# Fixed engine queues, a later load of the weights, and unread matrix products in a fused Fourier-filter and gated-causal-convolution kernel

## The chip, the core and the metric

The kernel runs on one core of a Trainium2 chip. The metric is device time in microseconds (us) from the start to the end of the program, the median of the runs that were made. Five engines work side by side, each on its own instruction queue in the order written there: TensorE (PE, matrix products), VectorE (DVE), ScalarE (ACT), GpSimd (POOL, here mostly an issuer of loads) and SyncE (SP, here an issuer of stores and of transfers through a scratch in DRAM). An engine waits for another only where an instruction has to.

## The reference

`x` is 8 batches of 3200 rows by 256 channels in float32. First each channel is filtered along the rows in the frequency domain; then a causal convolution of five taps gives a gate that multiplies a projection.

```
X = rfft(x, axis=1);  y = irfft(X * (filt_r + 1j*filt_i), n=3200, axis=1)
gate = sigmoid(sum_k conv_w[k] * y[s-4+k])        # per channel, rows before 0 are zero
out  = (gate * (y @ w_val)) @ w_out               # 256 x 256 each
```

## The kernel before

The rows are split as 3200 = 100 x 32, and the transform is done by products with tables of sines that the kernel makes itself. The program is a list of small tasks, named here as in the code with batch `b` and part:

- `lx` (POOL, line 286) loads an eighth of a batch of x into one of ten buffers `xt`. `s1` (PE, line 548) is the first transform step, 8 per batch; `so` copies its result out of PSUM. `t` (DVE, line 567) transposes, 4 per batch.
- `s2` (PE, line 577) is the second step, 7 per batch; `xs` copies it out; `z` (DVE, line 593) multiplies by the filter tile `f_t`; `ia` (PE, line 608) goes back; `ue` copies it out to the tile `u`.
- Batch 0 (`TURN`) is then transposed on DVE, `k` (line 649, 4 parts, output `vt`); the other batches go through a scratch in DRAM (`wr`, `lv` on SP, `escr`).
- `ib` (PE, line 659, 8 per batch) ends the inverse transform; `ye` (ACT, line 668) copies it to `yt`. Then for 7 blocks of rows: `cv` (convolution, PE, line 698 or 712), `ga` (sigmoid, ACT, line 722), `vl` (PE, line 732, with `wv_t`), `gv` (DVE, line 747), `op` (PE, line 755, with `wo_t`), `oe` (copy), `st` (store, SP, line 770).
- Once, at the start: `wd`, `wa` make the table `w_t`; `tp` (PE, line 455) and `te` make `a_t` and `b_t` from it, 4 and 8 tasks; `cid`, `cia`, `cim` make `ci_t`; `dg` makes the convolution's diagonals on ACT. The 24 transfers of the filter (`f_t`, lines 346 to 352) are followed by eight copies `fd`, which double it across partitions, four for its first part and four for its second.

The copies `so`, `xs`, `ue`, `oe`, `te` and `fd` can run on ACT (line 539, or 469) or on DVE (line 541). PSUM is one tile of four slots of two banks; a product into a slot waits until the slot's last content has been copied out.

What comes after what on an engine is decided while the program is built. `Plan` (line 126) holds for each task its engines with estimated costs, what it depends on, which buffers it takes and gives, and a rank from the list `TIMES`. `run` steps through an imagined time: whenever an engine is free it takes, among the tasks that are ready by the estimates, the one of the lowest rank (with an addition `STAY` where PE changes its kind of product, and `LEAN` where DVE takes a copy). The tasks are then emitted in that order under a manual schedule, so each engine's queue is fixed, and on the chip each instruction waits for its true inputs.

In that order POOL issues the loads of x for batch 0, those of the filter, the first load of batch 1 (`lx1,0`), then all eleven transfers of `wv_t` and `wo_t` (one task, `load_w`, line 356), and then the other loads of batch 1. PE has `s1` of batch 1's second eighth (`s11,1`) ahead of five of batch 0's seven `ia`.

Of the kernel before, what the change touches and what calls it, by code (L numbers as in the profile page):

```python
# [24 lines left out]
STAY, LEAN = 2.6, 5.1  # L25

TIMES = [6045, -2430, 3242, -301, 64, -3062, 3825, -4640, -1646, -3299, -5370, 2181, -2530, 351,
# [90 lines left out]
NCH = R // RC  # L118
# [7 lines left out]
class Plan:  # L126
# [17 lines left out]
    def run(self):  # L144
        left = dict(self.tasks)
        users, need = {}, {}
        for n, t in left.items():
            need[n] = len(t["deps"])
            for d in t["deps"]:
                users.setdefault(d, []).append(n)  # L150
# [75 lines left out]
def kernel(  # L226
# [51 lines left out]
    st = {}  # L278
# [668 lines left out]
```

## Time and profile before

| | us |
|---|---|
| median of 3 runs | 304.4 |
| lowest, highest of the 3 | 303.82, 306.0 |
| the profiled execution | 303.57 |
| its span, first to last instruction | 301.8 |
| PE, DVE, ACT, POOL busy in it | 258.3, 263.6, 256.2, 63.0 |

The profiled execution's time is 1.8 us longer than the span between its first and last instruction. The page gives busy time by engine for the whole span and in 40 slices of 7.5 us; other views give the instructions in order of time, the busy time in chosen stretches, and the chain of waits that ended last. Tiles are called by the program's names, so `xs<-ps` is the copy of a PSUM slot to `xs`. A timeline row is start, duration, engine, line, operation, output<-input, sizes and count, and in brackets the idle time before it with what ended it. In a timeline, merged rows of a count above one run from the first start to the last end.

### The profile page before, as it was taken

Reading aid. Unit: us, or ns where it says so; the run is one execution under the profiler, and the core shown is the slowest. Engines: PE = TensorE matmul, PEld = TensorE weight load, DVE = VectorE, ACT = ScalarE, POOL = GpSimd, SP = SyncE. Lnnn points to the kernel's source line nnn. Section 1 sums busy time; section 2 is a strip of 40 time slices with the busy share of each in tenths; the row PEclk is TensorE's granted clock in tenths of the full one; section 3 lists DMA queues with packets and bytes.
Section 4 is the critical chain, followed back from the end, with each engine's and each line's share of the span. In section 5 each row is a group of like instructions: output and inputs, shape, how many; then the busy total and the mean of one; then the engine's idle time right before and its main releaser. Section 6 shows DMA issues by size and latency. Waiting matters only on the chain.

```text
span 301.8 us, 9355 instructions
## 1 busy us (share of the span) xinstructions
PE 258.3 (86%) x3924; PEld 156.8 (52%) x3924; DVE 263.6 (87%) x294; ACT 256.2 (85%) x299; POOL 63.0 (21%) x122
## 2 busy tenths in 40 slices
PE   2822492778999899989999999999999999999991
PEld 0111340634555654666466465747666677766661
DVE  7979959898999999999999999999999984766761
ACT  3997775699789997999999999999999889787652
POOL 8699953022023002300320300000000000000000
PEclk9999998799999999999999999999999999999998
DMA  6998699469689997999999997998563799875375
GB/s 91 190 112 103 79 166 186 79 94 182 173 244 269 252 305 179 222 282 359 198 237 316 289 212 205 331 311 288 174 231 121 233 292 341 280 292 208 125 292 204
DMA packets 52874, 66.00 MB, mean 219 GB/s; under 512 B 7712, under 2 KB 34208, under 8 KB 52832
## 3 DMA queue, kind: packets, MB, share of 16 engines
q1 hardware_dynamic: 40624, 50.09, 49.2%
q0 software_dynamic: 12208, 15.31, 32.7%
q8 instruction: 31, 0.51, 0.7%
q14 instruction: 11, 0.09, 0.1%
HBM read 42.54 MB, written 38.14 MB: 267 GB/s over the span
## 4 chain that ended last, share of the span: by engine, by line
PE 48%; DMA 14%; DVE 14%; POOL 9%; ACT 8%; issue 6%; SPq 0%; DVEq 0%; POOLq 0%; ACTq 0%
PE ps L755 11%; PE ps L698 11%; PE ps L732 11%; DMA vt<-escr 8%; PE ps L659 5%; PE ps L608 4%; DVE gv L747 3%; DVE so L541 3%; PE ps L712 3%; DMA out_dram<-o 3%; DMA f_t<-in_filt_r_dram 2%; PE ps L548 2%; POOL xt L286 2%; ACT so L539 2%; DVE vt L649 2%
## 5 line engine op out<-in xcount | busy, mean ns | idle before, releaser
L747 DVE TENSOR_TENSOR gv<-ps,gt 128x1024 bf16<-128x1024 f32 (+1 forms) x56 | 60.8, 1103 | 13.5 <-PE ps L732 10.1
L593 DVE TENSOR_TENSOR z<-xs,f_t 128x2048 bf16<-128x2048 bf16 (+1 forms) x56 | 62.7, 1138 | 4.3 <-ACT xs L539 4.1
L722 ACT ACTIVATE gt<-ps 128x1024 bf16<-128x1024 f32 (+1 forms) x56 | 52.1, 945 | 10.4 <-PE ps L712 5.8
L286 POOL DMA_DIRECT2D xt<-in_x_dram x64 | 36.4, 570 | 108.6 <-PE ps L548 89.3
L668 ACT ACTIVATE yt<-ps 128x800 bf16<-128x800 f32 x64 | 52.1, 846 | 7.0 <-PE ps L659 6.5
L548 PE MATMUL ps<-xt,cf_t 100*128 100x512 bf16 x128 | 43.5, 424 | 11.6 <-DMA xt<-in_x_dram 9.3
L755 PE MATMUL ps<-wo_t,gv 128*128 128x256 bf16 x400 | 51.8, 273 | 0.8 <-DVE gv L747 0.4
L732 PE MATMUL ps<-yt,wv_t 128*128 128x512 bf16 (+1 forms) x224 | 51.9, 356 | 0.0
L698 PE MATMUL ps<-yt,dg_t 64*64 64x512 bf16 (+1 forms) x880 | 48.7, 348 | 0.4
L539 ACT ACTIVATE so<-ps 128x1024 bf16<-128x1024 f32 x42 | 42.2, 1042 | 6.6 <-PE ps L548 4.2
L539 ACT ACTIVATE u<-ps 128x1024 bf16<-128x1024 f32 (+1 forms) x41 | 40.0, 982 | 4.7 <-PE ps L608 4.3
L755 PEld LDWEIGHTS <-gv 128*128 128x128 bf16 x400 | 36.8, 97 | 12.2 <-issue 3.0
L539 ACT ACTIVATE o<-ps 128x1024 f32<-128x1024 f32 (+1 forms) x37 | 36.8, 999 | 6.2 <-PE ps L755 5.3
L659 PE MATMUL ps<-ci_t,vt 104*128 104x100 f16 (+1 forms) x512 | 33.7, 213 | 8.8 <-DVE vt L649 6.5
L567 DVE STREAM_TRANSPOSE tt<-so 128x1024 f32<-128x1024 f32 x32 | 38.7, 1227 | 0.6 <-ACT so L539 0.6
L539 ACT ACTIVATE xs<-ps 128x1024 bf16<-128x1024 f32 (+1 forms) x36 | 35.3, 998 | 3.6 <-PE ps L577 3.3
L659 PEld LDWEIGHTS <-vt 104*128 104x128 bf16 (+1 forms) x512 | 28.4, 101 | 19.0 <-DVE vt L649 7.1
L698 PEld LDWEIGHTS <-dg_t 64*64 64x64 bf16 x880 | 24.3, 106 | 15.4 <-issue 4.3
L608 PE MATMUL ps<-z,a_t 64*64 64x256 bf16 x416 | 28.4, 289 | 4.5 <-ACT gt L722 1.9
L577 PE MATMUL ps<-tt,w_t 64*64 64x256 bf16 x416 | 23.5, 293 | 9.4 <-DVE tt L567 8.5
L608 PE MATMUL ps<-z,b_t 64*64 64x256 bf16 x416 | 28.1, 283 | 0.0
L732 PEld LDWEIGHTS <-wv_t 128*128 128x128 bf16 x224 | 19.0, 97 | 17.3 <-issue 3.2
(98 smaller groups left out, 225.1 us busy)
## 6 DMA issues: line engine op xcount, KB each, us to landing
out_dram<-o SPq DMA_DIRECT2D x48, 512.0 KB
xt<-in_x_dram POOLq DMA_DIRECT2D x64, 200.0 KB, 7.3
escr<-u SPq DMA_DIRECT2D x42, 256.0 KB
vt<-escr SPq DMA_DIRECT2D x56, 192.0 KB
out_dram<-o SPq DMA_DIRECT2D x8, 128.0 KB
escr<-u SPq DMA_DIRECT2D x7, 128.0 KB
vt<-escr SPq DMA_DIRECT2D x56, 16.0 KB
f_t<-in_filt_r_dram POOLq DMA_DIRECT2D x2, 112.0 KB, 3.6
```

Source lines behind the costliest of these rows:

```text
L286: nc.gpsimd.dma_start(out=xt[0:L], in_=src)
L539: nc.scalar.activation(dst, src, AF.Copy, **kw)
L548: nc.tensor.matmul(ps[:, 512 * h:512 * h + 512], lhsT=cf_t[0:L].rearrange("p h c i -> p (h c i)"), rhs=xv[:, DQ // 2 * h:DQ // 2 * h + DQ ...
L593: nc.vector.tensor_tensor(z[:, :, :, 0:nm * D], st.pop(("XS", b, u))[:, :, 0:nm * D].unsqueeze(1) .to_broadcast((128, 2, 2, nm * D)), f_t[ ...
L608: nc.tensor.matmul(ps[64 * h:64 * h + 64, 512 * t + D * a:512 * t + D * a + D], lhsT=tab[rows, h, m0 + a, :], rhs=z[rows, w, h, D * a:D * ...
L659: nc.tensor.matmul(ps[:, o:o + L], lhsT=v[rows, RC * j + a, 128 * dh:128 * dh + 128], rhs=ci_t[rows, way, :], start=True, stop=True)
L668: nc.scalar.activation(y[:, :, H:H + N].rearrange("p h (a r) -> p h a r", r=R)[:, :, :, RC * j:RC * j + RC], ps[:, :].rearrange("p (h n) - ...
L698: nc.tensor.matmul(ps[o:o + 64, 512 * dh:512 * dh + w], lhsT=dg_t[rows, dh, k, :], rhs=y[rows, dh, BLK * c + k:BLK * c + k + w], start=(k ...
L722: nc.scalar.activation(g[:, :, 0:w], two_banks(ps, w), AF.Sigmoid)
L732: nc.tensor.matmul(ps[:, 512 * eh:512 * eh + w], lhsT=wv_t[:, dh, eh, o:o + 128], rhs=y[:, dh, H + BLK * c:H + BLK * c + w], start=(dh == ...
L747: nc.vector.tensor_tensor(o, i0, i1, op=ALU.mult)
L755: nc.tensor.matmul(ps[:, D * a:D * a + D], lhsT=gv_[:, eh, 128 * a:128 * a + 128], rhs=wo_t[:, c % 2 * pair(b, c), eh, :], start=(eh == 0) ...
```

## The change

The rank list goes. `QUEUES` now lists, for each of the five engines, the numbers of its tasks in order, so that both the order and the choice between ACT and DVE are written down. `run` only works out imagined times for that order, needed for the PSUM slots, and gives start and end of each task back. The core of it:

```diff
-TIMES = [6045, -2430, 3242, ...
+QUEUES = dict(
+    PE=[0, 2, 4, 6, 8, 10, 12, 1557, 14, 1554, 1563, 21, 1560, 26, 24, 31, 36, 29, 142, ...],
+    DVE=[1549, 1551, 1553, 1566, 16, 17, 18, 19, 1543, 1540, 1542, 23, ...],
...
+WARM, COLD = 0.25, (14.0, 45.0)
...
+            for e, line in lines.items():
+                if line and free.get(e, 0.0) <= now + 1e-9 and can(line[0]):
+                    begin(line.pop(0), e)
...
+            order.append((t["emit"], e, t["slots"], now, end))
...
-    def load_w():
+    def load_wv():
         for dh in range(2):
...
+
+    def load_wo():
         for s in range(2):
...
+    def warm(us):
+        flat = w_t[...].rearrange("p s k -> p (s k)")
+        ps = psum()
+        for h in range(int(us / WARM)):
+            o = 512 * (h % 2)
+            nc.tensor.matmul(ps[:, o:o + 512], lhsT=flat[:, 0:128],
+                             rhs=flat[:, o + 128:o + 640], start=True, stop=True)
...
-            dep = dep + ([f"s1{b},{j - 1}"] if j else [])
+            dep = dep + ([f"s1{b},{j - 1}"] if j else [f"s1{b - 1},{NCH - 1}"] if b else [])
...
-    add("wts", {"POOL": 5.0}, ["pool"], lambda e: load_w())
+    add("wv", {"POOL": 4.2}, ["pool"], lambda e: load_wv())
+    dma("wvq", 2.4, ["wv"], land=2.0, mode=1)
+    add("wo", {"POOL": 3.4}, ["wv"], lambda e: load_wo())
+    dma("woq", 2.6, ["wo"], land=2.0, mode=1)
...
-        for emit, e, slots in order:
+        idle = 0.0
+        for emit, e, slots, at, end in order:
+            st["slots"] = list(slots)
+            if e == "PE":
+                if slots and COLD[0] < idle and at < COLD[1] and at - idle > WARM:
+                    warm(at - idle)
+                idle = end
```

The estimates of when x, the filter and the loads arrive are changed too; they only enter the imagined times. The first `vl` and the first `op` now depend on the loads of `wv_t` and `wo_t` in the plan. No task is added or dropped; the only new instructions are the unread products.

**The unread products.** Where the plan leaves PE idle for over 0.25 us between its times 14 and 45, as many products of 128 x 512 as fit at 0.25 us each are put in front of the next task, in that task's PSUM slot, which they overwrite and which the task then overwrites. There are 54, each with a load of its stationary operand: 18 before `s20,0`, 9 before `ia0,0`, 4 before `ia0,1`, 2 before `s11,0`, 11 between `s20,4` and `s11,2` (1, 2, 2, 2, 1, 2, 1 before `s20,4`, `s20,5`, `s11,1`, `ia0,4`, `ia0,3`, `ia0,5`, `s11,2`), 3 before `s11,5` and 7 before `s11,6`. They read `w_t` alone.

**The first part of the queues**, from the transposes of batch 0 to the first `ib0`, before and after:

```
POOL before  lx1,0 [wv wo: 11 transfers] lx1,1 pd0 lx1,2 ... lx1,7 lx2,0 ... lx2,3 ha0 lx2,4 ...
POOL after   lx1,0 pd0 lx1,1 ... lx1,7 lx2,0 ... lx2,4 [wv: 4] lx2,5 lx2,6 ha0 lx2,7 [wo: 7] lx3,0 ...

DVE before   te3,0 fd0 t0 te1,0 fd0 t0 fd0 t0 fd1 cim t0 fd1 xs0,0 fd1 z0,0 z0,2 z0,1 ue0,2 z0,3
             z0,4 z0,5 so1,2 xs0,6 z0,6 so1,4 k0 k0 k0 k0 t1 t1 t1 t1
DVE after    t0 t0 t0 t0 fd0 fd0 fd0 z0,0 fd1 z0,1 z0,2 fd1 fd1 fd1 z0,4 z0,3 z0,5 z0,6 ue0,5
             k0 k0 k0 cim k0 t1 t1 t1 t1

ACT before   so0,6 te0,0 so0,7 so0,5 te3,1 te2,0 fd0 te1,1 dg0 cia te2,1 te0,1 fd1 xs0,2 so1,0
             xs0,1 ue0,0 xs0,3 xs0,4 ue0,1 xs0,5 so1,1 ue0,3 ue0,4 ue0,5 so1,3 ue0,6 so1 so1 so1 ye0
ACT after    so0,6 dg1 so0,5 so0,7 fd0 te1,0 te0,0 te1,1 te0,1 xs0,0 cia te2,0 xs0,1 te2,1 te3,0
             xs0,2 xs0,3 ue0,0 ue0,1 so1,0 xs0,4 xs0,5 te3,1 ue0,2 xs0,6 ue0,4 ue0,3 ue0,6 dg0
             so1 so1 so1 so1 so1 so1 so1 ye0

PE before    s20,0 s20,1 s11,0 s20,2 ia0,0 s20,3 ia0,2 s20,4 s11,1 ia0,1 s20,5 s11,2 ia0,3 s20,6
             ia0,4 ia0,5 s11,3 s11,4 ia0,6 s11,5 s11,6 s11,7 ib0
PE after     s20,0 tp2 s20,1 ia0,0 s20,2 s20,3 ia0,1 s11,0 ia0,2 s20,4 s20,5 s11,1 ia0,4 s20,6
             ia0,3 ia0,5 ia0,6 s11,2 s11,3 s11,4 s11,5 s11,6 s11,7 ib0
```

Up to the first `ib0` PE has the same tasks in both (16 `s1`, 7 `s2`, 7 `ia`, 4 `tp`), and from there on the same 372. Behind its last `k0` part DVE has 20 `so`, 18 `xs`, 14 `ue` and 19 `oe` before, and 12, 18, 17 and 19 after: five copies fewer, which ACT has more. The later orders differ in many places on all engines.

More of the change, by code (lines that the diff above doesn't have):

```diff
@@ L126, with __init__ @@
 class Plan:
-    def __init__(self, room, slots, times, stay=1.0, lean=0.0):
-        self.tasks, self.room, self.stay = {}, dict(room), stay
-        self.lean, self.slots, self.times = lean, list(range(slots)), iter(times)
+    def __init__(self, room, slots, queues):
+        self.tasks, self.room, self.queues = {}, dict(room), queues
+        self.slots = list(range(slots))
     def add(self, name, engines, deps, emit, take=(), give=(), land=0.0, mode=None,
             ps=0, free=()):
-        queue = engines.keys() - {"none", "DQ"}
-        rank = next(self.times) / 100 if queue else 0.0
-        self.tasks[name] = dict(engines=engines, rank=rank, deps=deps, emit=emit, take=take,
+        self.tasks[name] = dict(engines=engines, deps=deps, emit=emit, take=take,
                                 give=give, land=land, mode=mode, ps=ps, free=free, slots=[],
@@ L144, in run @@
     def run(self):
-        left = dict(self.tasks)
+        names = list(self.tasks)
+        lines = {e: [names[i] for i in q] for e, q in self.queues.items()}
         users, need = {}, {}
-        for n, t in left.items():
+        for n, t in self.tasks.items():
             need[n] = len(t["deps"])
@@ L150, in run, with can, begin @@
                 users.setdefault(d, []).append(n)
-        ready_at = {n: 0.0 for n in left}
-        free = {}
+        ready_at = {n: 0.0 for n in names}
+        loose = {e: [n for n in names if e in self.tasks[n]["engines"] and need[n] == 0]
+                 for e in ("none", "DQ")}
+        free, gives, order = {}, [], []
         mode = turn = None
-        gives = []
-        ready = {n for n in left if need[n] == 0}
-        order = []
-        now = 0.0
+        now, left = 0.0, len(names)
+        def can(n):
+            t = self.tasks[n]
+            return (need[n] == 0 and ready_at[n] <= now + 1e-9 and len(self.slots) >= t["ps"]
+                    and all(self.room[p] >= t["take"].count(p) for p in t["take"]))
+        def begin(n, e):
+            nonlocal mode, turn, left
+            t = self.tasks[n]
+            cost = t["engines"][e]
+            for p in t["take"]:
+                self.room[p] -= 1
+            t["slots"] = [self.slots.pop(0) for _ in range(t["ps"])]
+            if e == "PE":
+                cost += 0.1 if t["mode"] != mode else 0.0
+                mode = t["mode"]
+            if e == "DQ":
+                turn = t["mode"]
+            end = now + cost
+            done = end + SEM.get(e, 0.1)
+            if e != "none":
+                free[e] = end
+            back = list(t["give"]) + [self.tasks[o]["slots"][i] for o, i in t["free"]]
+            if back:
+                gives.append((done, back))
+            for u in users.get(n, ()):
+                need[u] -= 1
+                ready_at[u] = max(ready_at[u], done + t["land"])
+                for k in loose:
+                    if need[u] == 0 and k in self.tasks[u]["engines"]:
+                        loose[k].append(u)
+            left -= 1
+            order.append((t["emit"], e, t["slots"], now, end))
         while left:
@@ L190, in run @@
-            if best is None:
-                later = [ready_at[n] for n in ready if ready_at[n] > now + 1e-9]
-                later += [v for v in free.values() if v > now + 1e-9]
-                later += [g[0] for g in gives if g[0] > now + 1e-9]
-                assert later, ("stuck", sorted(ready)[:20], self.room)
-                now = min(later)
-                continue
-            _, n, e, cost = best
-            t = left.pop(n)
-            ready.discard(n)
-            for p in t["take"]:
-                self.room[p] -= 1
@@ L202, in run @@
-            t["slots"] = [self.slots.pop(0) for _ in range(t["ps"])]
-            if e == "PE":
-                if t["mode"] != mode:
-                    cost += 0.1
-                mode = t["mode"]
-            if e == "DQ":
-                turn = t["mode"]
-            end = now + cost
-            free[e] = end
-            done = end + SEM.get(e, 0.1)
-            back = list(t["give"]) + [self.tasks[o]["slots"][i] for o, i in t["free"]]
-            if back:
-                gives.append((done, back))
@@ L215, in run @@
-            for u in users.get(n, ()):
-                need[u] -= 1
-                ready_at[u] = max(ready_at[u], done + t["land"])
-                if need[u] == 0:
-                    ready.add(u)
-            order.append((t["emit"], e, t["slots"]))
+            went = left
+            for n in [n for n in loose["none"] if can(n)]:
+                if can(n):
+                    loose["none"].remove(n)
+                    begin(n, "none")
+            if left < went:
+                continue
@@ new lines, in run @@
+            for e, line in lines.items():
+                if line and free.get(e, 0.0) <= now + 1e-9 and can(line[0]):
+                    begin(line.pop(0), e)
+            if free.get("DQ", 0.0) <= now + 1e-9:
+                here = [n for n in loose["DQ"] if can(n)]
+                if here:
+                    n = min(here, key=lambda n: (
+                        round(ready_at[n] + (1e4 if self.tasks[n]["mode"] == turn else 0.0), 6),
+                        self.tasks[n]["at"]))
+                    loose["DQ"].remove(n)
+                    begin(n, "DQ")
@@ L221, in run @@
+            if left < went:
+                continue
+            later = [v for v in free.values() if v > now + 1e-9] + [g[0] for g in gives]
+            later += [ready_at[n] for n in loose["none"] + loose["DQ"]]
+            later += [ready_at[line[0]] for line in lines.values() if line and need[line[0]] == 0]
+            later = [v for v in later if v > now + 1e-9]
+            assert later, ("stuck", {e: line[:1] for e, line in lines.items()}, self.room)
+            now = min(later)
         self.span = max(free.values())
@@ L772, in store @@
             in_=o[:, 0:w // 128 * D])
[L775 to L776 removed]
+    plan = Plan(dict(xt=NXT, so=1, t=1, xs=3, z=3, u=1, e=2, v=1, y=2, g=NGB, gv=NGB, o=NOB), 4, QUEUES)
     add = plan.add
```

47 lines of the change are left out of this document (13 added, 34 removed), and 159 rows, old and new, of tables (ACT, DVE, PE, POOL).

## The prediction

> **What bounds the kernel now.** I read the busy shares in 40 slices first, then chosen stretches.
>
> ```profile
> PE   2822492778999899989999999999999999999991
> DVE  7979959898999999999999999999999984766761
> ACT  3997775699789997999999999999999889787652
> ```
> ```profile
> 50.18:57.01 6.83, 3.10 (x36) 2.94 (x37) 6.83 (x6) 2.03 (x3) 0.00 (x0) 0.50 0.86 159
> ...
> 60.00:210.00 150.00, 142.32 (x2092) 83.89 (x2087) 146.16 (x135) 140.97 (x164) 21.48 (x42) 1.00 0.92 246
> 210.00:290.00 80.00, 79.97 (x1496) 54.32 (x1486) 63.92 (x62) 67.46 (x78) 0.32 (x3) 1.00 0.67 235
> ```
>
> The second block's columns are length, then busy time (and count) of PE, weight loads, DVE, ACT and POOL, the granted clock and DMA. Three regimes show. From 60 to 210 us DVE (146.16 of 150) and ACT (140.97) are nearly full and PE idles only 7.7. From 210 to 290 PE is full (79.97 of 80). Up to 60 nothing is full, and that is where the change works. So the chain of waits there comes next:
>
> ```profile
> 24.50 1.33 POOL xt L286
> 25.82 0.75 POOL wv_t L359
> ...
> 32.96 0.51 POOL wo_t L367
> ...
> 33.63 3.67 DMA xt<-in_x_dram
> ...
> 37.35 1.03 PE ps L548 x2
> ...
> 40.35 1.03 ACT xs L539
> ...
> 41.41 0.04 DVE z L593
> ...
> 48.72 5.42 DVE vt L649 x3
> ...
> 54.18 3.22 PE ps L659 x39
> ```
>
> POOL issues the first x load of batch 1, then weights from 25.82 to 33.47, and only then the second x load, which lands at 37.30. `s11,1` waits for it, and behind it in PE's queue stand five of batch 0's seven `ia`. What they feed reaches DVE late, and `k`, which needs every `ue` of batch 0, ends just ahead of the first full `ib` (54.18). DVE's own timeline shows what it does meanwhile:
>
> ```profile
> 18.20 1.25 DVE L567 STREAM_TRANSPOSE tt<-so 128x1024 f32<-128x1024 f32 x1 [0.58 <-ACT so L539]
> 19.37 0.65 DVE L541 CAST a_t<-ps 128x512 f16<-128x512 f32 x1
> ...
> 22.39 0.95 DVE L541 COPY f_t<-f_t 32x3072 bf16<-32x3072 bf16 x1
> ...
> 25.72 0.46 DVE L303 TENSOR_SCALAR ci_t<-sx,wt 128x100 f16<-128x100 f32 x2
> ...
> 29.73 1.08 DVE L541 COPY f_t<-f_t 32x3584 bf16<-32x3584 bf16 x1
> ...
> 34.76 1.22 DVE L541 CAST u<-ps 128x1024 bf16<-128x1024 f32 x1
> 35.90 2.35 DVE L593 TENSOR_TENSOR z<-xs,f_t 128x2048 bf16<-128x2048 bf16 x2
> 41.41 1.23 DVE L593 TENSOR_TENSOR z<-xs,f_t 128x2048 bf16<-128x2048 bf16 x1 [3.16 <-ACT xs L539]
> 42.55 1.22 DVE L541 CAST so<-ps 128x1024 bf16<-128x1024 f32 x1
> 43.68 0.68 DVE L541 CAST xs<-ps 128x512 bf16<-128x512 f32 x1
> 44.40 0.69 DVE L593 TENSOR_TENSOR z<-xs,f_t 128x1024 bf16<-128x1024 bf16 x1
> ...
> 46.90 7.22 DVE L649 STREAM_TRANSPOSE vt<-u 128x1024 f32<-128x1024 f32 x4 [0.44 <-ACT u L539]
> 54.02 4.58 DVE L567 STREAM_TRANSPOSE tt<-so 128x1024 f32<-128x1024 f32 x4
> ```
>
> The 3.16 before 41.41 is the late x load's mark; the rest of DVE's time to 46.90 is work, part of it copies that another engine could do. `k` ends at 46.90 + 7.22 = 54.12.
>
> **Weights behind batch 1's x.** The 7.8 us of issuing (25.82 to 33.63) leave the path, and `s11,1` no longer holds up `ia`. They now stand behind `lx2,4`, which waits for `s11,2` to free a buffer, so around 40 us; on POOL they hold up `lx2,5` onwards, `ha0` and the loads of batch 3. Their first reader, and PE's full rate, are in this row (four products of 128 x 512 in 1.04, 0.26 each):
>
> ```profile
> 73.08 1.04 PE L732 MATMUL ps<-yt,wv_t 128*128 128x512 bf16 x4
> ```
>
> Even 7 us earlier it comes 15 us after all is issued: I cost it at nothing. The pad memset `pd0` moves one load up and is covered the same way, and the new dependency of `s1` on the batch before it costs nothing, being PE's own order.
>
> **DVE's queue up to `k`.** Off it go two `te`, two `xs`, two `so`; one `fd` comes. ACT takes what DVE sheds, and the order puts the four transposes first. DVE in the new order: four `t` at 4.58 / 4 = 1.15, so 4.6; three `fd` at 1.0, 3.0; four `fd` at 1.09, 4.4; six `z` at 2.35 / 2 and one of 0.69, 7.7; one `ue`, 1.2. The sum is 20.9. The start: ACT no longer does `te0,0` (0.58, next fence) ahead of the last `so0`, but takes `so0,0` after `so0,3`, one eviction of 0.93 moved behind waits for x, so the transposes start at about 18.2 + 0.3 = 18.5. DVE is then through at 39.4. ACT has this to do in between:
>
> ```profile
> 15.76 0.58 ACT L539 ACTIVATE a_t<-ps 128x512 f16<-128x512 f32 x1
> ...
> 18.94 2.76 ACT L539 ACTIVATE f_t<-f_t 32x3072 bf16<-32x3072 bf16 x1
> ...
> 23.50 0.35 ACT L312 ACTIVATE sx<-fyx 128x200 f32<-128x200 f32 x1
> ...
> 46.18 0.62 ACT L539 ACTIVATE u<-ps 128x512 bf16<-128x512 f32 x1
> 46.66 2.89 ACT L539 ACTIVATE so<-ps 128x1024 bf16<-128x1024 f32 x3
> ```
>
> From 18.5 to `ue0,6`: one `fd` 2.8, eight `te` about 4.7, `cia` 0.35, twelve copies at 0.93 (2.89 / 3 rounded down for overlap), 11.2, two half ones 1.1: 20.2, through at 38.7. The two queues are of equal length, so each now waits for the other in places. No row shows how much; nothing and the 3.6 us that DVE waited before (3.16 + 0.44) are the bounds, and I take 0.9, nearer to nothing, because no load stands behind it any more. `k` starts at 40.3 and with `cim` inside (0.46) ends at 40.3 + 7.2 + 0.5 = 48.0 against 54.12: **6.1 us earlier**, 7.0 without any wait. The x loads allow it: without weights between them those of batch 1 are issued back to back from 24.5, the second at about 26 instead of 33.63.
>
> **The unread products.** The cover for them is time in which PE waits. They cost where they run longer than that.
>
> ```profile
> 29.07 1.03 PE L548 MATMUL ps<-xt,cf_t 100*128 100x512 bf16 x2 [0.63 <-DMA xt<-in_x_dram]
> ```
> ```profile
> 146.02 0.61 PE L548 MATMUL ps<-xt,cf_t 100*128 100x512 bf16 x2
> ```
>
> The same pair takes 1.03 at 29 us and 0.61 later: in the first part PE runs at half rate, though the clock column says 1.00 there and 0.50 only at 50.18 to 57.01. So a product is 0.26 fast and up to 0.5 slow. The 18 before `s20,0` write the slot that the last `so0` frees, so they start at 18.5. In the window row at 50.18, full rate came back 2.8 us after `ib` began (57.01 - 54.18). By that the burst is six slow and twelve fast products, 18.5 + 3.0 + 3.1 = 24.6; without any release 27.5. `z0,0` cannot start before DVE's three `fd`, at 18.5 + 4.6 + 3.0 = 26.1, and needs `s20,0`, a copy of 1.0 and hops, 1.8 together: a burst that ends by 24.3 is free. So 0.3 late, which is inside the 0.9. The nine before `ia0,0` take 2.3 and lie while `z0,0` runs; the small groups wait for a slot that ACT frees and push PE by 0.2 to 0.5 each, while ACT, not PE, sets the pace. The last ten stand before x products of batch 1 that nothing needs before `k` ends.
>
> The Trainium skill's page "TensorE: Matmul & The Clock Gate" says in Part 1 that the array runs at half rate until one window of about 3.4 us has been busy; with that the burst would end at about 18.5 + 3.5 + 2.9 = 24.9, 0.6 late instead of 0.3, and the halved and full pairs above agree with it. It also says there that "the ramp penalty is <1% of a typical kernel span": 1% of this span is 3.0 us, and that speaks against paying 54 products for it. I book no gain for the clock in either case, since DVE and ACT set the pace to 48 us.
>
> **From there to the end.** From 54.18 to the last copy PE has 372 tasks, the same ones after, and the end is
>
> ```profile
> 294.46 2.10 ACT L539 ACTIVATE o<-ps 128x1024 f32<-128x1024 f32 x2 [1.53 <-PE ps L755]
> ```
>
> that is 296.56, and 5.2 us for the last store. The 242.4 us are carried over whole if the later order is as good. Known of it: ACT has five copies more (5 x 0.93 = 4.7), DVE five fewer. Set into the stretch of 150 us, ACT would have 145.7 and DVE about 140: the fuller engine stays at 146. So the loss is between nothing and 4.7, and a gain of up to PE's 7.7 us of idle cannot be excluded, though with DVE at 97% and ACT at 94% I see no room for most of it. I take a loss of 1.7, a third of the bound. **Sum:** -6.1 + 1.7 = -4.4. The span goes from 301.8 to 297.4, the profiled execution's 303.57 to 299.2, and since the median of the runs is 0.8 above that execution, 304.4 to **300.0**.
>
> **The rivals.** *The whole of it arrives*: no waits (7.0) and no later loss: 304.4 - 7.0 = 297.4. For it speaks that no engine's sum grows above DVE's of before; against, that DVE and ACT then each wait for the other's results with queues of equal length. *ACT takes over*: of 6.1 the moved copies eat 4.7, 303.0, no change to speak of. For it: ACT at 140.97 of 150 has no more than 9 us of room, and a fixed order gives an engine nothing else to do while it waits. *The unread products lie on the path*, slower: if the 54 run at 0.5 throughout, the burst ends at 27.5 (3.2 late), the nine take 4.5 from 29.3, while `z0,0` would be done by 30.5 (3.3 late), and the sixteen next exceed their gaps by a quarter us each (4.0): 10.5 on the 7.0 without waits and 1.7 later, 304.4 + 5.2 = 309.6. It decides where the mean product takes some 0.4 us; against it stand the return of full rate after 2.8 us and that 36 of the 54 stand behind the burst, where PE has been at work for longer than that. That the change doesn't do what it says can hardly be: the queues are written out, and the weights have 15 us to spare.
>
> **The numbers.** About 1% (3 us) can be told from no change; three runs spread over 0.7%. Forecast 0.52, with 298.2 to 302 of its own (waits of nothing to 2.7); whole gain 0.18; ACT 0.22; products 0.08. Faster by over 1% (below 301.4): most of the forecast and the second, 0.67. Within 1%: the ACT case and the forecast's upper end, 0.25. Slower: 0.08. The range leaves out the products' case and the edges of the others: 296.5, a little below the whole gain, to 303.8, a little above the ACT case.
>
> **What would show it.** Right: no idle DVE row of 3 us before 41, `k` starting at 39.5 to 41.5, the first full run of L659 near 48, and the 242.4 us behind it grown by 0 to 4. A burst of 18 that ends after 25.5, or L548 pairs of 1.03 behind it, speaks for the products; a later stretch in which ACT is over 98% busy and DVE waits for ACT speaks for the second rival. Wrong would be an L659 start after 51, or a later part longer by over 5 us.

## The result, and the profile after

| | before | after |
|---|---|---|
| median of 20 runs each, us | 305.06 | 302.28 |
| lowest, highest | 303.82, 306.19 | 300.65, 305.75 |
| the profiled execution | 303.57 | 302.18 |
| its span | 301.8 | 300.0 |
| end of the last `k0` part | 54.12 | 49.47 |
| end of the last copy of the output | 296.56 | 295.77 |
| from the one to the other | 242.44 | 246.30 |
| from there to the end of the span | 5.20 | 4.25 |

The ratio is 0.9916, with an interval of 0.9894 to 0.9938; the medians lie 2.8 us apart. That is faster by less than 1%. The three differences of the profiled executions are -4.65 (first part), +3.86 (later part) and -0.95 (last store), together -1.74 of span. So the first part gained most of what was forecast, and the later part gave most of it back.

This sum is that of two executions, and it is smaller than what the medians show. Their times differ by 1.39 us (the program ends 1.8 us after the span before and 2.2 after, so that only 0.60 of the last 0.95 reaches the time), the medians by 2.78. The execution of the kernel before that was profiled was 1.5 below its median; that of the changed kernel sits at its median. Where the other executions of the kernel before spend their 1.5 us, no trace shows. The first part may therefore have gained somewhat more than 4.65, or the later part lost somewhat less than 3.86.

The first part comes first. This is DVE's timeline of the changed kernel (start, duration, engine, line, operation, count, idle time before it). All its line numbers differ a little from those of before.

```profile
18.38 4.62 DVE L566 STREAM_TRANSPOSE tt<-so 128x1024 f32<-128x1024 f32 x4 [3.17 <-ACT so L538]
...
23.04 2.97 DVE L540 COPY f_t<-f_t 32x3072 bf16<-32x3072 bf16 x1
26.04 1.83 DVE L540 COPY f_t<-f_t 32x3072 bf16<-32x3072 bf16 x2
...
27.96 1.22 DVE L592 TENSOR_TENSOR z<-xs,f_t 128x2048 bf16<-128x2048 bf16 x1
...
36.11 4.10 DVE L592 TENSOR_TENSOR z<-xs,f_t 128x2048 bf16<-128x2048 bf16 x4 [0.17 <-ACT xs L538]
40.34 1.22 DVE L540 CAST u<-ps 128x1024 bf16<-128x1024 f32 x1
41.69 5.57 DVE L648 STREAM_TRANSPOSE vt<-u 128x1024 f32<-128x1024 f32 x3
...
47.51 1.96 DVE L648 STREAM_TRANSPOSE vt<-u 128x1024 f32<-128x1024 f32 x1
```

The 3.16 us of idle time are gone: from 18.38 to the start of `k` the timeline names one wait, of 0.17, and all DVE's gaps together are 0.72 us (busy 22.59 of 23.31). `k` starts at 41.69, just outside the 39.5 to 41.5 that was to show the step right. One row is out of line: the first filter copy takes 2.97, and the two behind it 1.83 together. POOL's timeline shows what ran beside it:

```profile
23.79 1.40 POOL L623 MEMSET u<- 128x1536 bf16 x1
25.11 6.93 POOL L275 DMA_DIRECT2D xt<-in_x_dram  x9
...
42.49 0.76 POOL L348 DMA_DIRECT2D wv_t<-in_moe_w_val_dram  x1
```

This is the pad memset `pd0`. Moved one load up, it now runs while DVE copies the filter. Before, it ran at 34.17. The weights are issued from 42.49.

TensorE in the same stretch, with the burst of 18 unread products in the first row:

```profile
18.40 5.82 PE L517 MATMUL ps<-w_t 128*128 128x512 f16 x18 [0.59 <-ACT so L538]
24.15 0.41 PE L576 MATMUL ps<-tt,w_t 64*64 64x256 bf16 x8
...
33.16 0.61 PE L547 MATMUL ps<-xt,cf_t 100*128 100x512 bf16 x2
...
49.52 3.75 PE L658 MATMUL ps<-ci_t,vt 128*128 128x100 f16 x47 [1.67 <-DVE vt L648]
```

The burst ends at 24.2 and the x products behind it take 0.61 a pair, not 1.03: full rate is there from then on to the end of `k`. The first full `ib` starts at 49.52; from 49.3 to 52.7 the clock is at half, as it was from 50.18 to 57.01 before.

Now the later part. The stretches are set so that they begin with the end of `k` in each kernel: 155.88 us, and all to the last copy (columns as before: length, busy time and count of PE, weight loads, DVE, ACT, POOL, clock, DMA). Before:

```profile
54.12:210.00 155.88, 147.59 (x2157) 88.52 (x2161) 150.90 (x140) 145.84 (x170) 21.54 (x42) 0.99 0.90 239
54.12:296.60 242.48, 232.81 (x3683) 146.18 (x3683) 217.93 (x205) 218.21 (x252) 21.86 (x45) 0.99 0.82 238
```

After, with one short stretch of it:

```profile
155.00:166.00 11.00, 8.57 (x90) 4.54 (x89) 8.36 (x9) 7.22 (x9) 0.00 (x0) 0.84 0.91 287
...
49.47:205.35 155.88, 145.96 (x2065) 87.23 (x2066) 145.34 (x134) 145.57 (x169) 23.89 (x47) 0.98 0.86 225
49.47:295.80 246.33, 234.97 (x3683) 147.58 (x3683) 214.20 (x199) 222.17 (x258) 24.20 (x50) 0.99 0.82 237
```

PE has the same 3683 matmuls in both. It is busy 2.16 us longer with them (234.97 against 232.81) and idle 1.69 longer (11.36 against 9.67). In the first 155.88 us it gets through 92 matmuls fewer, while ACT is no busier (145.57 against 145.84) and DVE less so. Much of it lies in 11 us: between 155 and 166 PE idles 2.43 and the clock is 0.84. The chain of waits there:

```profile
149.84 0.84 SPq L769
...
151.27 0.90 SPq L640
152.17 0.05 issue
152.22 8.41 DMA vt<-escr
160.63 0.14 issue
160.77 0.96 PE ps L658 x16
```

A load of batch 3's scratch (`vt<-escr`) is issued on SP behind stores of the output (L769), and 8.41 us pass until it has landed. TensorE waits for it until 160.77, and at 162.0 the clock falls to half for 3.4 us.

### The profile page after: what moved, and what is told of

Read it like the earlier page. It is cut to its first block, busy times and chain, and to the rows that moved or that the text cites. A ratio compares the mean times of both kernels' runs of the same rounds, so it can differ in the third digit from the quotient of the medians.

```text
span 300.0 us, 9422 instructions
## 1 busy us (share of the span) xinstructions
PE 269.2 (90%) x3978; PEld 161.0 (54%) x3978; DVE 257.5 (86%) x284; ACT 261.0 (87%) x309; POOL 61.7 (21%) x122
## 4 chain that ended last, share of the span: by engine, by line
PE 63%; ACT 15%; DVE 11%; DMA 5%; issue 3%; POOL 1%; SPq 1%; DVEq 0%; ACTq 0%; POOLq 0%
PE ps L731 13%; PE ps L754 12%; PE ps L697 12%; PE ps L607 6%; PE ps L547 5%; ACT so L538 5%; PE ps L658 5%; PE ps L517 4%; PE ps L576 3%; DVE gv L746 3%; ACT xs L538 3%; DMA vt<-escr 3%; DVE z L592 3%; PE ps L711 3%; DVE tt L566 2%
## 5 line engine op out<-in xcount | busy, mean ns | idle before, releaser
L275 POOL DMA_DIRECT2D xt<-in_x_dram x64 | 37.9, 595 | 105.9 <-PE ps L547 102.8
L538 ACT ACTIVATE so<-ps 128x1024 bf16<-128x1024 f32 x52 | 52.0, 1038 | 6.2 <-PE ps L547 5.8
L667 ACT ACTIVATE yt<-ps 128x800 bf16<-128x800 f32 x64 | 51.6, 849 | 3.9 <-PE ps L658 3.6
L731 PE MATMUL ps<-yt,wv_t 128*128 128x512 bf16 (+1 forms) x224 | 53.5, 363 | 0.7 <-ACT xs L538 0.7
L547 PE MATMUL ps<-xt,cf_t 100*128 100x512 bf16 x128 | 41.6, 414 | 7.0 <-DMA xt<-in_x_dram 5.8
L538 ACT ACTIVATE xs<-ps 128x1024 bf16<-128x1024 f32 (+1 forms) x38 | 37.3, 1000 | 4.9 <-PE ps L576 4.9
L538 ACT ACTIVATE o<-ps 128x1024 f32<-128x1024 f32 (+1 forms) x37 | 35.4, 962 | 5.3 <-PE ps L754 3.9
L538 ACT ACTIVATE u<-ps 128x1024 bf16<-128x1024 f32 (+1 forms) x38 | 36.8, 978 | 2.5 <-PE ps L607 2.4
L607 PE MATMUL ps<-z,a_t 64*64 64x256 bf16 x416 | 27.2, 280 | 3.0 <-DVE z L592 2.1
L540 DVE COPY o<-ps 128x1024 f32<-128x1024 f32 (+1 forms) x19 | 20.0, 1050 | 8.0 <-PE ps L754 5.8
L607 PE MATMUL ps<-z,b_t 64*64 64x256 bf16 x416 | 26.6, 272 | 0.0
```

Of the source, the lines that this page charges most:

```text
L538: nc.scalar.activation(dst, src, AF.Copy, **kw)
L547: nc.tensor.matmul(ps[:, 512 * h:512 * h + 512], lhsT=cf_t[0:L].rearrange("p h c i -> p (h c i)"), rhs=xv[:, DQ // 2 * h:DQ // 2 * h + DQ ...
L607: nc.tensor.matmul(ps[64 * h:64 * h + 64, 512 * t + D * a:512 * t + D * a + D], lhsT=tab[rows, h, m0 + a, :], rhs=z[rows, w, h, D * a:D * ...
L667: nc.scalar.activation(y[:, :, H:H + N].rearrange("p h (a r) -> p h a r", r=R)[:, :, :, RC * j:RC * j + RC], ps[:, :].rearrange("p (h n) - ...
L731: nc.tensor.matmul(ps[:, 512 * eh:512 * eh + w], lhsT=wv_t[:, dh, eh, o:o + 128], rhs=y[:, dh, H + BLK * c:H + BLK * c + w], start=(dh == ...
```

## The experiments

The first theory on the later loss is a new wait, that of `ib` for batch 3's scratch loads, with the half clock behind it. Against it stands the prediction's reason, ACT's added copies, by which the loss would be spread over the stretch. For the first part the theory is that the memset stole 2 us from the filter copies. In each expectation below, A is the explanation that was held likeliest for that run. All eleven runs are in one table. They were made in three groups, each on another chip and beside new runs of the kernel before, with medians of 304.43 (no_unread, scratch_order, memset_later, first_part_alone), 305.29 (later_order_alone, first_double, changed_again) and 305.30 (the others). So the ratios compare kernels of different groups better than the medians do. The last three columns are of one profiled execution each: the end of the last `k0` part, from there to the last copy, and whether the clock fell to half between 60 us and the last copies.

| | median | ratio, interval | end of `k` | rest | half clock |
|---|---|---|---|---|---|
| before | 305.06 | 1 | 54.12 | 242.44 | no |
| after | 302.28 | 0.9916 [0.9894, 0.9938] | 49.47 | 246.30 | at 162.0 |
| changed_again | 302.77 | one run | 49.79 | 246.57 | at 161.8 |
| no_unread | 303.57 | 0.9972 [0.9945, 0.9998] | 50.00 | 246.70 | at 160.5 |
| scratch_order | 301.11 | 0.9896 [0.9860, 0.9932] | 49.10 | 244.15 | no |
| memset_later | 302.03 | 0.9915 [0.9885, 0.9945] | 48.10 | 247.76 | at 161.5 |
| first_part_alone | 298.60 | 0.9802 [0.9777, 0.9827] | 49.03 | 242.62 | no |
| first_memset | 297.66 | 0.9754 [0.9736, 0.9771] | 48.18 | 242.24 | no |
| first_no_unread | 300.00 | 0.9825 [0.9803, 0.9847] | 50.38 | 243.17 | no |
| first_weights_front | 302.78 | 0.9882 [0.9840, 0.9925] | 53.27 | 243.10 | no |
| first_double | 307.92 | 1.0091 [1.0060, 1.0122] | 56.88 | 244.31 | no |
| before_weights_later | 302.67 | 0.9924 [0.9900, 0.9949] | 52.00 | 243.06 | no |
| later_order_alone | 308.12 | 1.0097 [1.0062, 1.0132] | 54.80 | 245.78 | no |

**The scratch loads.** In SP's queue two of batch 3's loads that come late change places with two that come early; nothing else moves.

```diff
-    586, 610, 299, 648, 642, 633, 630, 776, 119, 326, 317, 784, 636, 639, 800, ...
+    586, 610, 299, 636, 639, 633, 630, 776, 119, 326, 317, 784, 648, 642, 800, ...
```

> Only SyncE's order of batch 3's eight loads from the scratch is changed: parts 2 and 3 change places with 6 and 4, so parts 0 to 3 stand ahead of three stores. Theory A (the gain of the first part is given back by TensorE's wait for parts 2 and 3 at 158 us and by the half clock after it): no wait of TensorE over 1 us for vt near 158, no half clock between 60 and 290, the time 299.5 to 301.5, ratio 0.980 to 0.988, and the spread over the rounds under 2 us instead of 5. Theory C (the later order as a whole, ScalarE's five more copies, gives it back): the wait is gone but the time stays at 302 to 303.

```profile
155.00:166.00 11.00, 9.78 (x124) 5.44 (x122) 11.00 (x11) 9.85 (x13) 1.11 (x2) 1.00 0.97 302
...
49.10:293.30 244.20, 233.46 (x3683) 146.82 (x3683) 213.94 (x199) 222.45 (x258) 24.21 (x50) 0.99 0.82 239
```

These are stretches of this kernel. In the same 11 us PE now gets through 124 matmuls instead of 90, at full clock, and no wait for scratch is left; the longest one there is for DVE:

```profile
159.49 0.51 PE L658 MATMUL ps<-ci_t,vt 104*128 104x100 f16 x8 [0.93 <-DVE gv L746]
```

The rest is 244.15, 2.2 us shorter than in the changed kernel. So in the profiled pair the order of four entries in SP's queue was worth about 2.2 of the 3.86. The other runs bear this out in part only: the medians differ by 1.2, the ratios (0.9916 and 0.9896, the latter just outside the range expected) by 0.6 us, and their intervals overlap. The spread of the runs (299.65 to 303.8) did not shrink as expected, and the profiled execution was the shortest of the six.

Nor is it always the scratch that TensorE waits for. In no_unread (below), whose SP queue is that of the changed kernel, a half clock at the same place follows waits of 1.80 and 0.96 us, and the chain behind the second leads through a copy on ACT to a store of the output:

```profile
149.20 10.15 DMA out_dram<-o
```

The transfers of this stretch, loads and stores, keep the DMA engines 0.88 to 0.97 busy in the three kernels, and which of them TensorE waits for differs. In the profiled pair 1.7 us of the loss remain, with PE busy 0.65 and idle 1.07 longer than before the change. ACT's 222.45 is 4.2 above the 218.21 of before, as its added copies must make it, but nothing here shows that PE waits for them.

**The memset behind batch 1's loads.** It is issued after `lx1,6`:

```diff
         st["X", b, j] = xt
+        if b == 1 and j == NCH - 2:
+            nc.gpsimd.memset(st["U", 0][:, NS:32, :], 0.0)
...
     def pad(b):
         st["U", b] = upool.tile([128, 32, D], BF16, name="u")
-        if b in TURN:
-            nc.gpsimd.memset(st["U", b][:, NS:32, :], 0.0)
```

> GpSimd's memset of the pad of batch 0 is issued after the seventh x load of batch 1 instead of after the first, the rest as changed. Theory A (the memset held up VectorE's first filter copy, 2.97 us where others take 0.95): the first copy after the transposes takes 0.95 to 1.3, z of part 0 starts at 26.0 to 26.8 instead of 27.96, k ends 1 to 2 us earlier than 49.5, and the time is 0.5 to 2 us below the changed kernel's 302.3 (the wait at 158 us may still take some of it). Rival (the copy was held up by descriptor writing of the x loads or by TensorE's reads): the first copy still takes over 2 us and the time stays.

Its DVE timeline:

```profile
22.98 2.81 DVE L542 COPY f_t<-f_t 32x3072 bf16<-32x3072 bf16 x3
25.88 1.23 DVE L594 TENSOR_TENSOR z<-xs,f_t 128x2048 bf16<-128x2048 bf16 x1
27.14 1.84 DVE L542 COPY f_t<-f_t 32x3584 bf16<-32x3584 bf16 x1
...
46.12 1.98 DVE L648 STREAM_TRANSPOSE vt<-u 128x1024 f32<-128x1024 f32 x1
```

The three copies take 2.81 in place of 4.83, and `k` ends 1.37 earlier. A later copy took 1.84 instead of 1.08; POOL's record puts the memset at 29.09, just behind it, and spans on POOL are rough, so what slowed this copy isn't shown. But the time is that of the changed kernel (ratios of 0.9915 and 0.9916), not 0.5 to 2 us below it: TensorE resumes behind the scratch load at 160.78 here and at 160.77 there. What the first part gains is waited away at that load. The load was issued about 1 us earlier here (its two halves at 150.11 and 151.49, against 151.27 and 152.22) and landed no earlier, so its time of issue alone doesn't set when it lands.

**The products taken out, and nothing else** (`COLD` closed):

```diff
-WARM, COLD = 0.25, (14.0, 45.0)
+WARM, COLD = 0.25, (14.0, 0.0)
```

> The changed kernel without its 54 unread products (the first part's gaps stay empty). Theory A (the gain is the x loads and VectorE's shorter queue; the clock matters little): s2 and ia of batch 0 run at half rate again, the end of the k transposes moves by no more than 1 us either way (48.5 to 50.5 in the span), and the time is 301 to 303.5, ratio to the kernel before 0.988 to 0.996. Theory B (the products' full clock is the gain): k ends 3 us later or more, the time is back at 304.5 to 306.

`k` ends 0.53 later and the median is 1.3 above that of the changed kernel, 1.7 by the ratios, whose intervals just fail to overlap. The range expected for the time was missed by a hair. Without the products the pairs of x products are slow:

```profile
23.28 0.64 PE L576 MATMUL ps<-tt,w_t 64*64 64x256 bf16 x8 [5.25 <-DVE tt L566]
...
32.69 1.04 PE L547 MATMUL ps<-xt,cf_t 100*128 100x512 bf16 x2
```

DVE's timeline of this kernel, with the three filter copies that the memset slows, a wait for PE ahead of its `ue`, and the end of `k`:

```profile
23.26 4.45 DVE L540 COPY f_t<-f_t 32x3072 bf16<-32x3072 bf16 x3
...
40.92 1.23 DVE L540 CAST u<-ps 128x1024 bf16<-128x1024 f32 x1 [0.57 <-PE ps L607]
...
48.04 1.96 DVE L648 STREAM_TRANSPOSE vt<-u 128x1024 f32<-128x1024 f32 x1
```

From the end of these copies (27.71) to the end of `k` (50.00) it takes 22.29 us. In the changed kernel the same way takes 21.60 (27.87 to 49.47): 0.7 us for the products. At the end of `k` 0.53 of it is left, since the transposes began 0.22 later and the three copies took 0.38 less.

**The first part alone.** All queues of the changed kernel up to the last `k0`, the first `ib` and the first `ye` (POOL's up to the loads of `wo_t`), then the order of before on every engine. PE's joint, as an example:

```diff
     166, 170, 60, 62, 64, 66, 68, 70,
-    177, 340, 185, 72, 193, 344, 348, 352, 180, 201, 188, 209, 356, 196, 74, ...
+    72, 74, 340, 177, 185, 193, 344, 86, 348, 180, 352, 188, 356, 201, 360, ...
```

> Queues put together from both kernels: up to the last k, first ib and first ye as changed (weights later, unread products, new order), from there on the order of the kernel before on all engines, the choice between ScalarE and VectorE too. Theory A (the first part's 4.6 us are carried whole by the old later order): 300 to 301.5, ratio 0.983 to 0.988. Theory D (what is won in the first part is lost later whatever the order, because VectorE is full from 60 to 210 us): 303.5 to 305.

Its stretch from the end of `k` to the last copy:

```profile
49.03:291.70 242.67, 231.68 (x3683) 145.13 (x3683) 218.18 (x205) 218.15 (x253) 24.20 (x50) 1.00 0.83 240
```

242.62 against 242.44 before: the whole gain of the first part arrives at the end. The median of 298.6 us is 3.7 below that of the changed kernel (3.5 by the ratios) and better than the 300 to 301.5 expected. The old later order holds the earlier start without loss; the new one does not. In this execution the clock didn't fall at the first `ib`; in first_memset, with the same order, it was at half from 49.7 to 53.2, and the rest is 242.24. So the half clock there is not what sets the two orders apart.

**The later order alone.** The reverse: before's first part, the weights in front, no products, and the changed kernel's order behind it.

```diff
-    ..., 54, 150, 154, 158, 162, 166, 170, 60, 62, 64, 66, 68, 70, 177, 340, 185, 72, ...
+    ..., 49, 154, 158, 54, 162, 166, 170, 60, 62, 64, 66, 68, 70, 177, 340, 185, 72, ...
```

> The other half put together: up to the last k, first ib and first ye the queues of the kernel before (weights in front, no unread products), from there on the changed order. Theory A (the changed later order is worse by 1.7 us plus TensorE's wait for batch 3's scratch loads): from the end of k to the last copy 244 to 247 us against 242.4, the time 305.5 to 309. Rival (the later order is as good, and only fits badly behind the earlier first part): 242 to 243.5, 304 to 305.5.

1% slower than before. Its rest is 245.78, 3.34 above before, without any half clock after 60 us; TensorE's rows show smaller waits at the same tasks:

```profile
162.54 1.02 PE L733 MATMUL ps<-yt,wv_t 128*128 128x512 bf16 x4 [1.35 <-DVE o L542]
...
167.07 1.05 PE L660 MATMUL ps<-ci_t,vt 104*128 104x100 f16 x16 [1.15 <-DMA vt<-escr]
```

So the new later order is worse by some 3.3 us even where `k` ends late.

**Weights moved in the kernel before, and put back in front in the new first part.** In both, only the place of their issue on POOL changes:

```diff
 order = plan.run()
+spot = [i for i, o in enumerate(order) if o[0] is plan.tasks["wts"]["emit"]][0]
+moved = order.pop(spot)
+spot = [i for i, o in enumerate(order) if o[0] is plan.tasks["lx2,3"]["emit"]][0]
+order.insert(spot + 1, moved)
```

> The kernel before with one edit: the eleven transfers of the weights are issued after the fourth x load of batch 2 instead of after the first of batch 1; every other order as before, no unread products. Theory A (the late x load held up batch 0): VectorE's 3.16 us idle before the z at 41.41 is gone, k ends 2.5 to 3.5 us earlier than 54.12, the time is 2 to 3.5 us less, ratio 0.988 to 0.994. Rival (what VectorE's new order and ScalarE's copies save is the whole gain, the x wait is hidden anyway): k ends at 53 to 54.5 and the time is the same.

```diff
 order = plan.run()
+loads = [o for n in ("wv", "wo") for o in order if o[0] is plan.tasks[n]["emit"]]
+order = [o for o in order if o not in loads]
+spot = [i for i, o in enumerate(order) if o[0] is plan.tasks["lx1,0"]["emit"]][0]
+order[spot + 1:spot + 1] = loads
```

> The kernel put together from the changed first part and the old later order (298.6 us), with the weights' eleven transfers back in front of the second x load of batch 1, the rest unchanged. Theory A: the second s1 of batch 1 waits for its x until 35 to 37 us, five of batch 0's ia stand behind it, k ends 2 to 4 us later than 49.0, the time is 300.5 to 302.5. Rival (the new order has room for late x loads): k ends within 1 us of 49.0, 298 to 299.5.

In the kernel before the move brings 2.1 us at `k`; the 3.16 of idle time are gone. Its DVE timeline:

```profile
25.97 1.61 DVE L303 TENSOR_SCALAR ci_t<-sx,wt 128x100 f16<-128x100 f32 x2
...
44.77 7.22 DVE L649 STREAM_TRANSPOSE vt<-u 128x1024 f32<-128x1024 f32 x4 [0.32 <-ACT u L539]
```

The two small `ci_t` took 0.46 before; the memset, which the shorter queue brings forward to 26.07, lies right there. Without these 1.15 us `k` would have ended about 3.3 earlier than before (an estimate: 2.12 + 1.15), inside the 2.5 to 3.5 expected. With the weights in front of the new first part, TensorE waits for the second load of batch 1 again, and longer than before:

```profile
38.92 0.67 PE L549 MATMUL ps<-xt,cf_t 100*128 100x512 bf16 x2 [3.71 <-DMA xt<-in_x_dram]
```

`k` ends 4.24 later than in first_part_alone, and the median is 4.2 higher, 2.4 by the ratios (0.9882 against 0.9802, intervals apart); its six runs lie between 299.65 and 303.48, the profiled one at 303.33. Wait, `k` and median all came out a little above the ranges expected. The weights' place and the new queues need each other: 2.1 of the 5.09 us (54.12 to 49.03) come from the weights alone in the old order, 4.24 are lost in the new one if they stay in front.

**Products: none, 54, and 108**, all with the old later order. The first is the edit of `COLD` above; the other:

```diff
-        for h in range(int(us / WARM)):
+        for h in range(2 * int(us / WARM)):
```

> The same put-together kernel (298.6 us) without the 54 unread products. Theory A (TensorE's clock in the first part is worth little, since VectorE and ScalarE set the pace): k ends 0 to 1 us later than 49.0, 298.5 to 300. Theory B (the products are worth a good part of the gain): k ends 2 us later or more, over 300.5. Theory E (they cost more than they bring): k earlier, under 298.3.

> The put-together kernel of 298.6 us with twice as many unread products, 108. The burst before s20,0 gets 36 products, at least 22 of them at full rate. Theory A (products cost only where they run longer than the wait that covers them): the burst ends 3.5 to 5 us later, near 28, z of part 0 starts 1.5 to 3 us later, the later groups add some, k ends 2.5 to 6 us later than 49.0, the time is 301 to 305. Rival (TensorE has room throughout the first part): k ends within 1 us, 298 to 299.5.

The medians are 300.0, 298.6 and 307.9, the ratios 0.9825, 0.9802 and 1.0091. Without the products `k` ends 1.35 later, between what Theory A (0 to 1) and Theory B (2 or more) said. The medians differ by 1.4, the ratios by 0.7 us with intervals that overlap (0.9803 to 0.9827), so a gain in the time is likely rather than shown. At `k` it is shown: from the end of the three filter copies to the end of `k` first_no_unread takes 22.28 us (28.10 to 50.38) and first_part_alone 21.62 (27.41 to 49.03), the same 0.7 as in the pair above; the rest of the 1.35 is a later start of the transposes (19.01 against 18.54) and a slower first copy. Doubled, the products cost about 9 us, more than either theory allowed. TensorE and then DVE of the doubled kernel:

```profile
18.98 9.16 PE L519 MATMUL ps<-w_t 128*128 128x512 f16 x36 [0.59 <-ACT so L540]
...
29.61 4.04 PE L519 MATMUL ps<-w_t 128*128 128x512 f16 x18 [0.69 <-ACT xs L540]
```
```profile
29.59 1.23 DVE L594 TENSOR_TENSOR z<-xs,f_t 128x2048 bf16<-128x2048 bf16 x1 [1.70 <-ACT xs L540]
...
35.54 1.22 DVE L594 TENSOR_TENSOR z<-xs,f_t 128x2048 bf16<-128x2048 bf16 x1 [2.35 <-ACT xs L540]
```

The burst now ends at 28.1, behind the filter copies (27.9), and DVE waits for what comes of it; the 18 in front of the first `ia` do the same at 35.54. In the prediction, the rival that put the products on the path had this mechanism; 54 products did not set it off.

**The memset ahead of everything, with the first part alone**: put among the filter's loads, at 12.25 us.

```diff
+                if m0 == 0 and f is filt_r:
+                    st["U", 0] = upool.tile([128, 32, D], BF16, name="u")
+                    nc.gpsimd.memset(st["U", 0][:, NS:32, :], 0.0)
...
     def pad(b):
-        st["U", b] = upool.tile([128, 32, D], BF16, name="u")
-        if b in TURN:
-            nc.gpsimd.memset(st["U", b][:, NS:32, :], 0.0)
+        if b not in TURN:
+            st["U", b] = upool.tile([128, 32, D], BF16, name="u")
```

> The same put-together kernel (298.6 us) with GpSimd's memset of the pad of batch 0 issued among the filter's loads, after the first six of them, where VectorE has small operations only. Theory A (the later order carries what the first part wins, and the memset cost the first filter copy up to 2 us): the three first filter copies take 0.95 to 1.1 each, none of the four others over 1.2, k ends at 47.2 to 48.2 instead of 49.0, the time is 296.8 to 298, ratio 0.975 to 0.979. Rival (that time is lost again behind k): k earlier, time 298.3 to 299.

Its DVE timeline:

```profile
23.30 2.81 DVE L545 COPY f_t<-f_t 32x3072 bf16<-32x3072 bf16 x3
26.21 1.23 DVE L597 TENSOR_TENSOR z<-xs,f_t 128x2048 bf16<-128x2048 bf16 x1
...
40.45 5.55 DVE L652 STREAM_TRANSPOSE vt<-u 128x1024 f32<-128x1024 f32 x3
...
46.23 1.95 DVE L652 STREAM_TRANSPOSE vt<-u 128x1024 f32<-128x1024 f32 x1
```

No copy is slow any more, `k` starts at 40.45 and ends at 48.18. The median is 297.66, 2.5% below the kernel before and the fastest of all; the interval of its ratio lies just below that of first_part_alone.

**The changed kernel once more**, unedited, to see whether its wait comes back at the same place.

> The changed kernel once more, for one more profiled execution. Theory A (its runs spread from 300.65 to 305.75 because the wait for batch 3's scratch loads at 158 us and the half clock behind it come in some executions and not in others): an execution of 301.7 or less has no TensorE wait of over 1.5 us there and no half clock between 60 and 290; one of 302 or more has both. Rival (the spread comes from the first part): the end of k differs by over 1.5 us from 49.5.

It does: 2.21 us of waiting for scratch up to 161.16, and the half clock from 161.8, while `k` ends within 0.32 us of the first time. But this execution took 302.77 and the first 302.18, so the other half of A, executions of up to 301.7 without the wait, is not tested. It may well hold: the eight runs of up to 301.63 have a mean granted clock of 0.989 to 0.991 against 0.986 and 0.985 in the two profiles, and 3.41 us at half rate in 300 are 0.006 of the mean.

## Why the prediction was right, and where not

The direction was right, and 302.28 is inside the range; but the forecast's -4.4 came out as -2.8, which falls into the band within 1% that had 0.25. Both large terms of its sum were mis-sized, and in the same direction: as the two profiled executions show them, they add up to -0.8 (-4.65 + 3.86). That the medians moved by 2.8 all the same, and that the time came out near the forecast's own 298.2 to 302, is partly luck: 0.6 came from the last store, which the sum had at nothing, and 1.4 from the spread of the executions, since the profiled one of the kernel before lay 1.5 below its median.

- **First term, 6.1 us, measured 4.65.** The waits were estimated well (0.9 taken, 0.72 measured), and so was DVE's work, but for one row. The step that failed is the sentence on `pd0`: moved up one load, "covered the same way". It was costed by who waits for POOL, not by what runs beside it, and the filter copy beside it took 2.97 instead of 0.95. With the memset out of the way `k` starts at 40.45 and ends at 48.18; the forecast had 40.3 and 48.0.
- **Unread products, nothing, measured 0.5 at `k` and 1.3 in the median.** The burst was forecast to end at 24.6 and ended at 24.2. That it costs nothing was right. That the clock brings nothing "since DVE and ACT set the pace" was not: behind the filter copies `k` came 0.7 us sooner with the products, in both pairs. The Trainium skill's page "TensorE: Matmul & The Clock Gate", Part 1, was cited with a ramp penalty below 1%; 1.3 us is 0.4% (0.6% by the ratios), so the sentence held, and the products still paid a little.
- **Later loss, 1.7, measured 3.86.** "Carried over whole if the later order is as good" was the right condition, and it was not as good; the old order did carry the gain whole (242.62). The price was worked out from ACT's copies alone, and SP's queue was not looked through. There the scratch loads of batch 3 stood behind stores, and with four entries changed 2.2 of the 3.86 were gone in the profiled pair, though the medians don't show as much. That the new later order is the worse one is shown by later_order_alone and first_part_alone; what makes the other 1.7 is not settled; that it equals the forecast's figure does not show the forecast's reason.
- **The store at the end, nothing, measured -0.95.** It goes with the new later order: from the last copy to the end it is 4.2 to 4.7 us in all profiles with that order and 5.1 to 5.2 in all with the old one. As the program then ends later behind the span, 0.60 of it reached the time. The cause wasn't tried.
- **The rivals.** ACT did not take over: it is no busier in the 155.88 us behind `k`, and a wait for a DMA ends last. "The whole of it arrives", 297.4, is near what the first part does once the memset is moved and the old later order kept: 297.66. That the figures agree so well is partly luck, since `k` then ends 5.9 earlier, not 7.0, and the kernel before ran at 305.3 beside it, not at 304.4. The weights had room to spare as said: they are issued from 42.49 to 51.6, and the first product that reads them starts at 66.6.

## What to carry to other kernels

When a queue is shifted, look at every engine that shifts with it: price a moved instruction by what will run beside it, not only by who waits for it, and go through the store queue for loads that now stand behind large stores. A gain at the start is kept only if the order behind it still fits; joining the new first part to the old rest, which is cheap to try, separates the two. Filling idle TensorE time with unread products can pay a little, but doubling them cost about 9 us where the first 54 brought 0.7 at `k`.

## What was not expected of the hardware

- **A POOL memset beside a DVE copy.** In seven profiles the 32x3072 bf16 copy took 2.35 to 2.97 us beside a memset of 1.40, and 0.95 otherwise: longer by as much as the memset itself or more. It began 0.1 to 0.8 us ahead of the memset's record and ended 0.81 to 0.82 us behind the record's end in all seven, as if it had done its work after the memset. The Trainium skill's page "SBUF — State Buffer", section "SBUF: two separate sides", says that DVE in its two-port modes and GpSimd share a port pair that one of them holds for a whole instruction while the other blocks. The rows agree in kind: in the changed kernel a copy held up to the memset's recorded end (25.19) would end about 0.95 later, at 26.1, and it ended at 26.0. By POOL's record, though, the copy started first (23.04 against 23.79) and should have held the memset up; which of the two is at fault, the rule or that record, no run here tells.
- **The clock.** In the burst nine products took the first 3.6 us (0.40 each), the other nine 2.2. That is when full rate came, and the clock column shows 1.00 throughout: ahead of the first clock event in this trace, at 22.0, it says nothing. Later, a single wait of 2.43 us ahead of 160.77 was followed by half rate from 162.0 to 165.4, and so were waits of 2.21 and 1.92 at the same place in changed_again and memset_later, whereas the shorter waits of later_order_alone (1.35 and 1.15) were not. Each stretch of half rate in these profiles ahead of the last copies lasts 3.41 us or two or three times that, as the window of 3.4 us in Part 1 of the Trainium skill's page "TensorE: Matmul & The Clock Gate" would have it.
- **The spread.** The 20 runs of the changed kernel lie between 300.65 and 305.75. Those up to 301.63 had a mean granted clock of 0.989 to 0.991, those from 303.2 up 0.962 to 0.984. So the longer runs had more time at a lower clock; why that differs from run to run wasn't tried.
